# A windowed attention with sinks and a highway layer on one core: last batch loaded in single tokens, loads issued sooner, sinks' keys on GpSimd, sinks' scores in a values' bank, two stretches reordered

## The chip, the core and the metric

The kernel runs on one core of a Trainium2 chip. A core has five engines that matter here, each with an instruction queue of its own that is worked off in order: TensorE (PE in the profile, its weight loads PEld), VectorE (DVE), ScalarE (ACT), GpSimd (POOL) and SyncE (SP). Engines wait for one another by semaphores. Transfers go through 16 DMA engines; they are issued from SP's, ACT's or POOL's queue. The metric is the device time of one execution in microseconds (us); less is better.

## The reference, cut to what matters

Attention over 4 batches, 8 heads, 768 tokens, head size 64, with 4 sinks (the first four keys, which all queries see) and a window of 128 keys; its output, 3,072 tokens of 512 values, goes through a highway layer.

```python
scores = scale * np.matmul(q, k.transpose(0, 1, 3, 2))
keep = is_sink | in_window            # in_window: 0 <= query - key < 128
a = softmax(np.where(keep, scores, -1e9))
x = np.matmul(a, v)                   # then (batch, token) x (head, d): 3072 x 512
H = np.maximum(x @ w_h, 0.0)
T = 1.0 / (1.0 + np.exp(-(x @ w_t + b_t)))
return T * H + (1.0 - T) * x
```

## The kernel before

**Tiles.** 24 token tiles of 128, six for each batch b; tile n is tile t = n mod 6 of its batch. For each tile the work is a chain over engines:

- q and k come from memory by GpSimd's DMAs (`load_part`, L105), are made fp16 on the way, and lie in `nat` with a token per partition: a batch has two halves of 384 tokens, each with 4 loads of q and 4 of k (by groups of heads). In a load, a partition takes 12 tokens that follow one another. VectorE turns blocks of 32x32 (`transpose_qk`, L126), so that head dimension is on partitions: `tr`. As a partition has 12 neighbouring tokens, the result is written with a step of 12 elements between tokens.
- `scores(n)` (L235): TensorE, key tile n against query tiles n and n+1 (only n in a batch's last tile), 16 matmuls into four PSUM banks `ps_s`. `expo(n)` (L266): ScalarE, into E. `mask(n)` (L274): VectorE, in place.
- Tiles with t of 2 and more also need the sinks: `sink_keys(b)` (L215, VectorE, two instructions) puts a batch's first four keys in place, `sink_scores(n)` (L250) makes 4 matmuls of 128x128 into the first 128 columns of `ps_z` (for n of 3 and 4: `ps_h`), `sink_expo(n)` (L257) is ScalarE's exponential of them.
- `values(n)` (L289, L298, L301): TensorE, E times V for tiles n-1 and n, and the sinks, into `ps_v`, one PSUM tile of two banks of 512. `norm(n)` (L310, L311): VectorE, reciprocal of the sums and product: X, fp16.
- `x_transpose(n)` (L338): four TensorE transposes of X into bank 1 of `ps_v`; `x_copy(n)` (L343): ScalarE copies them to XT.
- `bias(n)` and `gate(n)` (L346, L350): TensorE into `ps_z`; `tanh(n)` (L367): ScalarE; the identity 0.5 x + 0.5 behind it on ScalarE for n below 16 and the last two tiles (`gate_on_act`, L373), on GpSimd for the others (`gate_value`, L378).
- `hidden(n)` (L383): TensorE into `ps_h`. `diff(n)` (L387) and `gated(n)` (L391): VectorE. `finish(n)` (L396): GpSimd adds X, and SP issues the store.

**The order.** It is written out by hand: the program's text is, for each engine, the order of its queue, and a dependency from each instruction to the one before it on its engine keeps it (`_keep_traced_order`, L19). Semaphores between engines are set by the framework from the tiles that instructions read and write. A stretch written out in full (L471 to L534) starts tiles 0 to 4. Then a loop (L535) of 20 turns, s from 2 to 21, has four tiles in flight: n2 = s+2 gets its scores, n1 = s+1 its values and norm, n0 = s its transposes, gate and hidden, n9 = s-1 its diff, gated and finish. A turn begins

```python
if n2 > 4:
    if n2 % NC >= 2:
        sink_scores(n2)
        sink_expo(n2)
    x_transpose(n0)
    x_copy(n0)
    scores(n2)
bias(n0)
```

and goes on with `expo(n2)`, `gate_value(n9)`, `diff(n9)`, `mask(n1)`, `gated(n9)`, `finish`, the turn's loads, its VectorE transposes of later q and k (`pieces`), `sink_keys` in a batch's first turn, the first half of the gate, `values(n1)`, `norm(n1)`, the second half, `tanh(n0)` and `hidden(n0)`. Turns in this text are named by n2: 4 to 23. What is loaded in which turn stands in the table `loads` (`put`, L436 to L444), what VectorE transposes in `transposed` (L417 to L422). A stretch after the loop (L574 to L604) ends tiles 21 to 23; the last one is worked in two halves of 256 columns.

Of the kernel before, what the change touches and what calls it, by code (L numbers as in the profile page):

```python
# [32 lines left out]
def kernel(  # L33
# [49 lines left out]


    SEG = 2 * P
    halves = [(0, S // 2), (S // 2, S // 2)]

    segments = [[[(0, SEG), (SEG, S - SEG)], [(0, SEG), (SEG, SEG), (2 * SEG, SEG)]]] + [
        [halves, halves] for b in range(1, B)]
    nat = [[[data.tile([P, HG, nt // 32, D], FP16, tag=f"nat{b}_{t0}_{w}",  # L90
                       name=f"nat{b}_{t0}_{w}") for t0, nt in segments[b][w]]
            for w in range(2)] for b in range(B)]
    tr = [data.tile([P, 2, HG, S, 2], FP16, tag=f"tr{b}", name=f"tr{b}")
          for b in range(B)]

# [9 lines left out]
    def load_part(b, i, g, which, into=None, engine=pool):  # L105
# [5 lines left out]
            in_=(q, k)[which][b, :, t0:t0 + nt, :].rearrange(  # L111
                "(g hg) (r m) d -> g r hg (m d)", g=G, m=nt // 32)[g])

    def part_loads(b, i, which):

        return [lambda g=g: load_part(b, i, g, which) for g in range(G)]

    def segment_loads(b, i):
        return part_loads(b, i, 0) + part_loads(b, i, 1)

    def transpose_qk(b, i, which, lo, hi):

        t0, nt = segments[b][which][i]
        dst = tr[b].bitcast(FP32).rearrange("p w hg t e -> p w hg (t e)")[
            :, which, :, t0:t0 + nt].rearrange("p hg (r m) -> p hg m r", m=nt // 32)
        dve.transpose(out=dst[:, :, lo:hi, :],  # L126
                      in_=nat[b][which][i].bitcast(FP32)[:, :, lo:hi, :])

    def load_v(n):
        b, t = divmod(n, NC)  # L130
# [79 lines left out]
                       base=NSINK - 1, pattern=[[NSINK, H]], channel_multiplier=-1)  # L210


    def sink_keys(b):
        for hg in range(HG):
            dve.tensor_tensor(  # L215
                out=sk[b][:, hg, :, 0:H * NSINK].rearrange("p e (h s) -> p e h s", s=NSINK),
                in0=tr[b][:, 1, hg, 0:NSINK, :].rearrange("p s e -> p e s").unsqueeze(2)
                .to_broadcast([P, 2, H, NSINK]),
                in1=skmask[:, hg].unsqueeze(1).unsqueeze(3)
                .to_broadcast([P, 2, H, NSINK]), op=ALU.mult)  # L220
# [18 lines left out]


    def sink_bank(n):
        return (ps_h if n in (3, 4) else ps_z)[:, 0:P]

    def sink_scores(n):
        b, t = divmod(n, NC)
# [38 lines left out]
    def values(n):  # L284
        b, t = divmod(n, NC)
        both = av_of(n)
        for i in range(2):
            if t >= 2:
                pe.matmul(both[:, i], lhsT=es[n % 2],  # L289
                          rhs=vs[b][:, HB * i:HB * i + HB, :].rearrange("p h e -> p (h e)"),  # L290
                          start=True, stop=False, skip_group_check=True)
            for j in range(HB):
                h = HB * i + j
                g, hg = divmod(h, HG)
                slot = both[:, i, j * (D + 1):(j + 1) * (D + 1)]
                first = t < 2 and j == 0
                if t > 0:
                    pe.matmul(slot, lhsT=E[n - 1][:, g, hg, P:2 * P], rhs=v_of(n - 1)[:, h, :],  # L298
                              start=first, stop=False, skip_group_check=True)
                    first = False  # L300
                pe.matmul(slot, lhsT=E[n][:, g, hg, 0:P], rhs=v_of(n)[:, h, :],  # L301
                          start=first, stop=True, skip_group_check=True)
# [33 lines left out]
    def x_transpose(n):  # L336
        for kc in range(KC):
            pe.transpose(xt_of(n)[:, kc * P:(kc + 1) * P], flat(X[n])[:, kc * P:(kc + 1) * P],  # L338
                         ident)

    def x_copy(n):
        XT[n] = work.tile([P, KC * P], FP16, tag="XT", name="XT")
        act.copy(out=XT[n], in_=xt_of(n))  # L343
# [4 lines left out]
    def gate(n, cols=ALL, parts=range(KC)):  # L348
        for kc in parts:
            pe.matmul(z_of(n, cols), lhsT=XT[n][:, kc * P:(kc + 1) * P], rhs=wt[:, kc, cols],  # L350
                      start=False, stop=(kc == KC - 1))
# [5 lines left out]
    def outputs(n):  # L357
        TH[n] = work.tile([P, DM], FP16, tag="TH", name="TH")
        DD[n] = work.tile([P, DM], FP16, tag="DD", name="DD")
        O[n] = work.tile([P, DM], FP32, tag="O", name="O")  # L360

    def on_act(n):

        return n < 16 or n >= N - 2

    def tanh(n, cols=ALL, gate_too=True):
        act.activation(out=TH[n][:, cols], in_=z_of(n, cols), func=AF.Tanh, scale=0.5)  # L367
        if gate_too:
            gate_on_act(n, cols)
# [11 lines left out]
    def hidden(n, cols=ALL):  # L381
        for kc in range(KC):
            pe.matmul(h_of(n, cols), lhsT=XT[n][:, kc * P:(kc + 1) * P], rhs=wh[:, kc, cols],  # L383
                      start=(kc == 0), stop=(kc == KC - 1))

    def diff(n, cols=ALL):
        dve.scalar_tensor_tensor(out=DD[n][:, cols], in0=h_of(n, cols), scalar=0.0,  # L387
                                 in1=flat(X[n])[:, cols], op0=ALU.max, op1=ALU.subtract)
# [2 lines left out]
        return dve.tensor_tensor(out=DD[n][:, cols], in0=DD[n][:, cols], in1=TH[n][:, cols],  # L391
                                 op=ALU.mult)

    def finish(n, cols=ALL, engine=pool, queue=sp, after=None):

        ins = engine.tensor_tensor(out=O[n][:, cols], in0=DD[n][:, cols],  # L396
                                   in1=flat(X[n])[:, cols], op=ALU.add)
        if after is not None:
            tc.add_manual_dep(
                ins.ins, after.ins.name,  # L400
                mybir.DependencyInfo(
                    mybir.DependencyClass.Sync, mybir.DependencyReason.DATA),
                reason="not beside it")
        queue.dma_start(out=out[n * P:(n + 1) * P, cols], in_=O[n][:, cols])

# [4 lines left out]
    def transposed(b, i, parts, steps):  # L412
        for part, n in zip(parts, steps):
            pieces[n] += [(b, i, *p) for p in part]
# [3 lines left out]
    transposed(1, 1, [[(0, 0, 8), (0, 8, 12)], [(1, 0, 8), (1, 8, 12)]], (7, 8))  # L418
    transposed(2, 0, half_1, (9, 10, 11))
    transposed(2, 1, half_2, (12, 13, 14))  # L420
    transposed(3, 0, half_1, (15, 16, 17))
    transposed(3, 1, half_2, (18, 19, 20))  # L422

    loads = {n: ([], []) for n in range(N)}

    def put(parts, counts):
        parts = list(parts)
        for n, behind, count in counts:
            for i in range(count):
                loads[n][behind].append(parts.pop(0))  # L430
        assert not parts
# [4 lines left out]
    loads[3][0].extend([lambda: load_v(4), lambda: load_v(5)])  # L436
    loads[4][1].append(lambda: load_v_heads(1, 0, H))
    put(segment_loads(1, 1), ((4, 1, 3), (5, 1, 3), (6, 1, 2)))
    put(segment_loads(2, 0), ((6, 1, 2), (7, 1, 4), (8, 1, 2)))
    put(v_halves(2), ((8, 1, 1), (9, 1, 1)))  # L440
    put(segment_loads(2, 1), ((9, 1, 2), (10, 1, 4), (11, 1, 2)))
    put(segment_loads(3, 0), ((11, 1, 2), (12, 1, 4), (13, 1, 2)))
    put(v_halves(3), ((13, 1, 1), (14, 1, 1)))
    put(segment_loads(3, 1), ((14, 1, 1), (15, 1, 4), (16, 1, 3)))  # L444

    loads[17][1].append(lambda: sink_values(3))

# [22 lines left out]

    dve.tensor_copy(out=nat[0][1][0], in_=first[1])  # L471
    transpose_qk(0, 0, 1, 0, 8)
    sink_keys(0)
    act.copy(out=nat[0][0][0][:, 1], in_=first[0][:, 1])
    dve.tensor_copy(out=nat[0][0][0][:, 0], in_=first[0][:, 0])
    transpose_qk(0, 0, 0, 0, 8)
# [40 lines left out]
    hidden(0)  # L517
    x_transpose(2)
    x_copy(2)
    diff(0)  # L520
    transpose_qk(0, 2, 1, 0, 8)
    gated(0)
    for load in loads[3][0]:
        load()
# [7 lines left out]
    expo(4)  # L532
    gate_on_act(1)
    hidden(1)  # L534
    for s in range(2, N - 2):  # L535

        n2, n1, n0, n9 = s + 2, s + 1, s, s - 1
        if n2 > 4:
            if n2 % NC >= 2:
                sink_scores(n2)  # L540
                sink_expo(n2)
            x_transpose(n0)
            x_copy(n0)
            scores(n2)
        bias(n0)
        if n2 > 4:
            expo(n2)
        gate_value(n9)
        diff(n9)
        if n1 > 3:  # L550
            mask(n1)
        last = gated(n9)
        for load in loads[n2][0]:
            load()
        for n in finished.get(n2, (n9,)):
            finish(n, after=last if n2 < 7 else None)
        for load in loads[n2][1]:
            load()
        for piece in pieces[n2]:
            transpose_qk(*piece)  # L560
        if n2 >= NC and n2 % NC == 0:
            sink_keys(n2 // NC)
        if n2 == N - 1:
            finish(n9, after=mask(n2))
        outputs(n0)

        gate(n0, parts=range(0, 2))
        values(n1)
        norm(n1)
        gate(n0, parts=range(2, KC))  # L570
        tanh(n0)
        hidden(n0)
# [14 lines left out]
    x_copy(n1)  # L587
    tanh(n0)
    hidden(n0)
    diff(n0)  # L590
    gated(n0)
    finish(n0)
    outputs(n1)
    for cols in HALVES:
        bias(n1, cols)
        gate(n1, cols)
        tanh(n1, cols)
    for cols in HALVES:
        hidden(n1, cols)
        diff(n1, cols)  # L600
    for cols in HALVES:
        gated(n1, cols)
    finish(n1, HALVES[0], engine=pool)
    finish(n1, HALVES[1], engine=dve, queue=act)  # L604

    _keep_traced_order(tc)
# [33 lines left out]
```

## Time and profile before

| what | value |
|---|---|
| median of 3 runs | 120.95 us (120.65 to 121.06) |
| the profiled execution, its own time | 120.54 us |
| its span, first to last instruction | 118.4 us |
| mean granted TensorE clock | 0.997 |
| busy: PE, DVE, ACT, POOL | 102.2, 98.3, 92.2, 84.5 us |
| DMA packets | 35,023, 17.52 MB; 26,433 of them under 512 B |
| queue of GpSimd's DMAs (q0) | 30,608 packets, 82.7% of 16 engines' span |
| one `x_copy` (L343), mean | 575 ns |
| one exponential of 128x2048 (L266), mean | 1,965 ns |
| one VectorE transpose of 128x512 and of 128x256 (L126), mean | 1,085 and 612 ns |
| issue of one q or k load, of one half of a batch's V, on GpSimd | about 0.55 and 1.44 us |

The span of the profile lies between the first and the last instruction; the execution's own time has some 2 us around it. A busy share is an average over stages with different limits, so what a stage is worth is read from the stage: from the chain of waits (the work that ended last, followed back), from the timeline of one engine in a stretch (start, duration, line; in brackets how long the engine was idle before and what ended that), and from tables of busy time for stretches. Ends of matmuls in the profile are modelled, and one group's end may lie up to 0.16 us behind the next one's start. The trace also has, for every load, the times at which it landed, and the packets of each DMA queue with their sizes.

### The profile page before, as it was taken

Reading aid. Unit: us, or ns where it says so; the run is one execution under the profiler, and the core shown is the slowest. Engines: PE = TensorE matmul, PEld = TensorE weight load, DVE = VectorE, ACT = ScalarE, POOL = GpSimd, SP = SyncE. Lnnn points to the kernel's source line nnn. Section 1 sums busy time; section 2 is a strip of 40 time slices with the busy share of each in tenths; the row PEclk is TensorE's granted clock in tenths of the full one; section 3 lists DMA queues with packets and bytes.
Section 4 is the critical chain, followed back from the end, with each engine's and each line's share of the span. In section 5 each row is a group of like instructions: output and inputs, shape, how many; then the busy total and the mean of one; then the engine's idle time right before and its main releaser. Section 6 shows DMA issues by size and latency. Waiting matters only on the chain.

```text
span 118.4 us, 3080 instructions
## 1 busy us (share of the span) xinstructions
PE 102.2 (86%) x1189; PEld 55.8 (47%) x1189; DVE 98.3 (83%) x194; ACT 92.2 (78%) x118; POOL 84.5 (71%) x119
## 2 busy tenths in 40 slices
PE   5987868879769879999997999999989999999910
PEld 1333445435435445556463454655544556555700
DVE  5679875846997899999979998999999996697580
ACT  0985789769649989999697999897969987863730
POOL 7969999699398996798789696975554435415360
PEclk9999999999999999999999999999999999999998
DMA  3999999999999999899999789999320222022132
GB/s 108 237 204 139 133 167 200 162 144 127 131 149 252 297 191 161 163 164 172 189 233 192 142 166 183 162 228 200 115 89 0 89 94 89 0 94 89 59 118 89
DMA packets 35023, 17.52 MB, mean 148 GB/s; under 512 B 26433, under 2 KB 31297, under 8 KB 35010
## 3 DMA queue, kind: packets, MB, share of 16 engines
q0 software_dynamic: 30608, 9.97, 82.7%
q1 hardware_dynamic: 3938, 6.72, 16.6%
q10 hardware_dynamic: 464, 0.66, 2.1%
q8 instruction: 9, 0.15, 0.5%
q14 instruction: 4, 0.03, 0.1%
HBM read 21.01 MB, written 6.29 MB: 231 GB/s over the span
## 4 chain that ended last, share of the span: by engine, by line
PE 37%; DMA 21%; DVE 16%; issue 8%; ACT 7%; POOL 6%; ACTq 1%; DVEq 0%
PE ps_z L350 9%; DMA wh<-in_moe_w_h_dram 8%; PE ps_h L383 7%; DMA nat<-in_q_dram 5%; DMA first<-in_q_dram 5%; DVE tr L126 4%; PE ps_s L235 4%; POOL nat L109 4%; DVE X L311 4%; ACT E L266 3%; PE ps_v L301 3%; DVE DD L387 3%; DMA v<-in_v_dram 3%; PE ps_v L338 3%; PE ps_z L346 2%
## 5 line engine op out<-in xcount | busy, mean ns | idle before, releaser
L266 ACT ACTIVATE E<-ps_s,ebias 128x2048 f16<-128x2048 f32 (+1 forms) x24 | 43.7, 1822 | 3.0 <-PE ps_s L235 3.0
L396 POOL TENSOR_TENSOR O<-DD,X 128x512 f32<-128x512 f16 (+1 forms) x24 | 27.2, 1135 | 24.3 <-DVE DD L391 12.7
L350 PE MATMUL ps_z<-wt,XT 128*128 128x512 f16 (+1 forms) x96 | 27.6, 375 | 0.3
L126 DVE STREAM_TRANSPOSE tr<-nat 128x512 f32<-128x512 f32 (+1 forms) x30 | 25.5, 896 | 0.8 <-DMA nat<-in_q_dram 0.6
L383 PE MATMUL ps_h<-wh,XT 128*128 128x512 f16 (+1 forms) x96 | 24.2, 375 | 0.4 <-DMA wh<-in_moe_w_h_dram 0.4
L274 DVE TENSOR_TENSOR E<-E,mask_std 128x2048 f16<-128x2048 f16 (+1 forms) x20 | 22.2, 1109 | 0.3 <-ACT E L266 0.2
L387 DVE SCALAR_TENSOR_TENSOR DD<-ps_h,X 128x512 f16<-128x512 f32 (+1 forms) x24 | 16.2, 676 | 4.8 <-PE ps_h L383 3.7
L367 ACT ACTIVATE TH<-ps_z 128x512 f16<-128x512 f32 (+1 forms) x24 | 14.0, 585 | 5.3 <-PE ps_z L350 4.9
L109 POOL DMA_DIRECT2D nat<-in_k_dram x32 | 17.7, 564 | 0.5 <-DMA v<-in_v_dram 0.5
L343 ACT COPY XT<-ps_v 128x512 f16<-128x512 f16 x23 | 13.2, 575 | 5.7 <-PE ps_v L338 5.7
L311 DVE TENSOR_TENSOR X<-ps_v,rec 128x512 f16<-128x512 f32 x23 | 15.9, 691 | 1.1
L109 POOL DMA_DIRECT2D nat<-in_q_dram x28 | 15.5, 560 | 1.2 <-DMA wh<-in_moe_w_h_dram 1.1
L235 PE MATMUL ps_s<-tr 32*128 32x256 f16 (+1 forms) x384 | 14.3, 264 | 2.1 <-DVE mask L477 1.0
L301 PE MATMUL ps_v<-v,E 128*128 128x65 f16 x184 | 15.4, 195 | 0.7 <-DVE E L274 0.6
L298 PE MATMUL ps_v<-v,E 128*128 128x65 f16 x152 | 15.0, 193 | 0.1
L383 PEld LDWEIGHTS <-XT 128*128 128x128 f16 x100 | 9.6, 98 | 11.0 <-issue 0.7
L301 PEld LDWEIGHTS <-E 128*128 128x128 f16 x192 | 12.2, 97 | 5.3 <-DVE E L274 3.7
L373 ACT ACTIVATE TH<-TH,half 128x512 f16<-128x512 f16 (+1 forms) x19 | 13.3, 699 | 0.6
L338 PE MATMUL ps_v<-ident,X 128*128 128x128 f16 x92 | 9.0, 220 | 5.5 <-DVE X L311 5.4
L298 PEld LDWEIGHTS <-E 128*128 128x128 f16 x160 | 12.5, 98 | 2.3 <-issue 0.2
L176 PE MATMUL ps_h<-zeros 128*128 128x512 f16 x36 | 10.3, 442 | 1.3 <-DVE zeros L179 1.3
L391 DVE TENSOR_TENSOR DD<-DD,TH 128x512 f16<-128x512 f16 (+1 forms) x25 | 10.4, 418 | 1.3 <-ACT TH L373 1.3
(70 smaller groups left out, 117.9 us busy)
## 6 DMA issues: line engine op xcount, KB each, us to landing
out_dram<-O SPq DMA_DIRECT2D x23, 256.0 KB, 3.6
nat<-in_q_dram POOLq DMA_DIRECT2D x24, 96.0 KB, 5.3
nat<-in_k_dram POOLq DMA_DIRECT2D x24, 96.0 KB, 4.1
v<-in_v_dram POOLq DMA_DIRECT2D x4, 384.0 KB, 7.8
v<-in_v_dram POOLq DMA_DIRECT2D x6, 128.0 KB, 5.2
v<-in_v_dram POOLq DMA_DIRECT2D x1, 768.0 KB, 10.7
nat<-in_q_dram POOLq DMA_DIRECT2D x4, 128.0 KB, 5.2
nat<-in_k_dram POOLq DMA_DIRECT2D x8, 64.0 KB, 6.9
```

The source lines that it names most:

```text
L109: engine.dma_start(out=into[32 * g:32 * g + 32].rearrange("p hg m d -> p hg (m d)"), in_=(q, k)[which][b, :, t0:t0 + nt, :].rearrange("(g ...
L126: dve.transpose(out=dst[:, :, lo:hi, :], in_=nat[b][which][i].bitcast(FP32)[:, :, lo:hi, :])
L235: pe.matmul(ps_s[:, g, hg, 0:nq * P], lhsT=tr[b][rows, 1, hg, c * P:(c + 1) * P, e], rhs=tr[b][rows, 0, hg, c * P:(c + nq) * P, e], start= ...
L266: act.activation(out=E[n][:, :, :, 0:nq * P], in_=ps_s[:, :, :, 0:nq * P], func=AF.Exp, bias=ebias, scale=SCALE)
L274: return dve.tensor_tensor(out=e3, in0=e3, in1=m[:, 0:nq * P].unsqueeze(1).to_broadcast([P, H, nq * P]), op=ALU.mult)
L298: pe.matmul(slot, lhsT=E[n - 1][:, g, hg, P:2 * P], rhs=v_of(n - 1)[:, h, :], start=first, stop=False, skip_group_check=True)
L301: pe.matmul(slot, lhsT=E[n][:, g, hg, 0:P], rhs=v_of(n)[:, h, :], start=first, stop=True, skip_group_check=True)
L311: dve.tensor_tensor(out=X[n], in0=av[:, :, :, 0:D], in1=rec.unsqueeze(3).to_broadcast([P, 2, HB, D]), op=ALU.mult)
L350: pe.matmul(z_of(n, cols), lhsT=XT[n][:, kc * P:(kc + 1) * P], rhs=wt[:, kc, cols], start=False, stop=(kc == KC - 1))
L383: pe.matmul(h_of(n, cols), lhsT=XT[n][:, kc * P:(kc + 1) * P], rhs=wh[:, kc, cols], start=(kc == 0), stop=(kc == KC - 1))
L387: dve.scalar_tensor_tensor(out=DD[n][:, cols], in0=h_of(n, cols), scalar=0.0, in1=flat(X[n])[:, cols], op0=ALU.max, op1=ALU.subtract)
L396: ins = engine.tensor_tensor(out=O[n][:, cols], in0=DD[n][:, cols], in1=flat(X[n])[:, cols], op=ALU.add)
```

## The change

- **Last batch in single tokens.** q and k of batch 3 no longer come in halves but in 8 loads (4 of q, 4 of k) into one tile `whole`; partition r of a group takes tokens r, r+32, r+64 and so on, so each load has 32 x 48 runs of 64 values instead of 32 x 2 of 768. VectorE transposes it by token tiles: `transpose_tile(n)`, one instruction of 128x512 for q and k of tile n, with neighbouring tokens written side by side. The first one waits for all 8 loads. They stand in turns 16 to 21 for tiles 18 to 23; before, there were four of 128x512 and four of 128x256 in turns 15 to 20.
- **Loads sooner.** In turns 7 to 13 more loads, and none of q or k behind turn 13 (table in the diff).
- **Sinks' keys** of batches 1 to 3 on GpSimd, behind the turn's `finish` and loads; those of batch 0 stay on VectorE.
- **Sinks' scores** of tiles from 5 on go to bank 0 of `ps_v`, and stand behind X's transposes and copy; those of 3 go to `ps_h`, of 2 and 4 to `ps_z`.
- **Fifth step** (turn 4 and what is ahead of it): two VectorE transposes and a norm move ahead of `diff(0)`, `diff(1)` and `gated(1)`.
- **End.** The identity of tile 22 goes to GpSimd; the last tile's second half loses its identity on ScalarE and is finished with two fused VectorE operations.

```diff
+    RUNS = B - 1
+    whole = data.tile([P, 2, HG, S // 32, D], FP16, tag="whole", name="whole")
...
+    def load_whole(g, which):
+        pool.dma_start(
+            out=whole[32 * g:32 * g + 32, which].rearrange("p hg m d -> p (hg m) d"),
+            in_=(q, k)[which][B - 1].rearrange(
+                "(g hg) (m r) d -> g r (hg m) d", g=G, r=32)[g])
...
+    def transpose_tile(n):
+        b, t = divmod(n, NC)
+        dst = tr[b].bitcast(FP32).rearrange("p w hg t e -> p (w hg) (t e)")
+        src = whole.bitcast(FP32).rearrange("p w hg m d -> p (w hg) (m d)")
+        dve.transpose(out=dst[:, :, t * P:(t + 1) * P], in_=src[:, :, t * P:(t + 1) * P])
...
-    def sink_keys(b):
+    def sink_keys(b, engine=pool):
         for hg in range(HG):
-            dve.tensor_tensor(
+            engine.tensor_tensor(
...
     def sink_bank(n):
-        return (ps_h if n in (3, 4) else ps_z)[:, 0:P]
+        return {2: ps_z, 3: ps_h, 4: ps_z}.get(n, ps_v[:, 0])[:, 0:P]
...
     def on_act(n):
-        return n < 16 or n >= N - 2
+        return n < 16 or n == N - 1
...
-    transposed(3, 0, half_1, (15, 16, 17))
-    transposed(3, 1, half_2, (18, 19, 20))
+    tiles = {n: [n + 2] for n in range(RUNS * NC - 2, N - 2)}
...
-    put(segment_loads(2, 0), ((6, 1, 2), (7, 1, 4), (8, 1, 2)))
+    put(segment_loads(2, 0), ((6, 1, 2), (7, 1, 5), (8, 1, 1)))
     put(v_halves(2), ((8, 1, 1), (9, 1, 1)))
-    put(segment_loads(2, 1), ((9, 1, 2), (10, 1, 4), (11, 1, 2)))
-    put(segment_loads(3, 0), ((11, 1, 2), (12, 1, 4), (13, 1, 2)))
+    put(segment_loads(2, 1), ((8, 1, 1), (9, 1, 2), (10, 1, 5)))
+    put([lambda which=which, g=g: load_whole(g, which)
+         for which in range(2) for g in range(G)], ((11, 1, 3), (12, 1, 3), (13, 1, 2)))
     put(v_halves(3), ((13, 1, 1), (14, 1, 1)))
-    put(segment_loads(3, 1), ((14, 1, 1), (15, 1, 4), (16, 1, 3)))
...
+    transpose_qk(0, 2, 1, 0, 8)
     diff(0)
-    transpose_qk(0, 2, 1, 0, 8)
     gated(0)
...
     hidden(1)
+    for piece in pieces[4]:
+        transpose_qk(*piece)
     for s in range(2, N - 2):
         n2, n1, n0, n9 = s + 2, s + 1, s, s - 1
         if n2 > 4:
+            x_transpose(n0)
+            x_copy(n0)
             if n2 % NC >= 2:
                 sink_scores(n2)
                 sink_expo(n2)
-            x_transpose(n0)
-            x_copy(n0)
             scores(n2)
...
         diff(n9)
-        if n1 > 3:
+        if n2 == 4:
+            outputs(n0)
+            gate(n0, parts=range(0, 2))
+            values(n1)
+            norm(n1)
+        else:
             mask(n1)
         last = gated(n9)
...
     hidden(n0)
+    gate_value(n0)
     diff(n0)
...
-    for cols in HALVES:
+    for i, cols in enumerate(HALVES):
         bias(n1, cols)
         gate(n1, cols)
-        tanh(n1, cols)
+        tanh(n1, cols, gate_too=(i == 0))
     for cols in HALVES:
         hidden(n1, cols)
-        diff(n1, cols)
-    for cols in HALVES:
-        gated(n1, cols)
-    finish(n1, HALVES[0], engine=pool)
-    finish(n1, HALVES[1], engine=dve, queue=act)
+    diff(n1, HALVES[0])
+    gated(n1, HALVES[0])
+    finish(n1, HALVES[0])
+    cols = HALVES[1]
+    diff(n1, cols)
+    dve.scalar_tensor_tensor(out=DD[n1][:, cols], in0=TH[n1][:, cols], scalar=1.0,
+                             in1=DD[n1][:, cols], op0=ALU.add, op1=ALU.mult)
+    dve.scalar_tensor_tensor(out=O[n1][:, cols], in0=DD[n1][:, cols], scalar=0.5,
+                             in1=flat(X[n1])[:, cols], op0=ALU.mult, op1=ALU.add)
+    act.dma_start(out=out[n1 * P:(n1 + 1) * P, cols], in_=O[n1][:, cols])
```

More of the change, by code (lines that the diff above doesn't have):

```diff
@@ L85 @@
     SEG = 2 * P
+    RUNS = B - 1
     halves = [(0, S // 2), (S // 2, S // 2)]
     segments = [[[(0, SEG), (SEG, S - SEG)], [(0, SEG), (SEG, SEG), (2 * SEG, SEG)]]] + [
-        [halves, halves] for b in range(1, B)]
+        [halves, halves] for b in range(1, RUNS)]
     nat = [[[data.tile([P, HG, nt // 32, D], FP16, tag=f"nat{b}_{t0}_{w}",
                        name=f"nat{b}_{t0}_{w}") for t0, nt in segments[b][w]]
-            for w in range(2)] for b in range(B)]
+            for w in range(2)] for b in range(RUNS)]
+    whole = data.tile([P, 2, HG, S // 32, D], FP16, tag="whole", name="whole")
     tr = [data.tile([P, 2, HG, S, 2], FP16, tag=f"tr{b}", name=f"tr{b}")
@@ L392, in gated, with finish @@
                                  op=ALU.mult)
-    def finish(n, cols=ALL, engine=pool, queue=sp, after=None):
-        ins = engine.tensor_tensor(out=O[n][:, cols], in0=DD[n][:, cols],
+    def finish(n, cols=ALL, after=None):
+        ins = pool.tensor_tensor(out=O[n][:, cols], in0=DD[n][:, cols],
                                    in1=flat(X[n])[:, cols], op=ALU.add)
@@ L403, in finish @@
                 reason="not beside it")
-        queue.dma_start(out=out[n * P:(n + 1) * P, cols], in_=O[n][:, cols])
+        sp.dma_start(out=out[n * P:(n + 1) * P, cols], in_=O[n][:, cols])
     half_1, half_2 = [[(0, 0, 8)], [(1, 0, 8)], [(0, 8, 12), (1, 8, 12)]], [
@@ L472 @@
     transpose_qk(0, 0, 1, 0, 8)
-    sink_keys(0)
+    sink_keys(0, engine=dve)
     act.copy(out=nat[0][0][0][:, 1], in_=first[0][:, 1])
@@ L558 @@
             load()
-        for piece in pieces[n2]:
-            transpose_qk(*piece)
+        if n2 > 4:
+            for piece in pieces[n2]:
+                transpose_qk(*piece)
+        for n in tiles.get(n2, ()):
+            transpose_tile(n)
         if n2 >= NC and n2 % NC == 0:
@@ L564 @@
             finish(n9, after=mask(n2))
[L565 to L569, printed above, removed]
+        if n2 > 4:
+            outputs(n0)
+            gate(n0, parts=range(0, 2))
+            values(n1)
+            norm(n1)
         gate(n0, parts=range(2, KC))
```

## The prediction

> **What bounds the kernel now.** I read the busy shares first (PE 86%, DVE 83%, ACT 78%): averages, which name no bound. Then the table of busy time for single turns of the loop. A turn is called by its newest token tile, n2; `hidden(n0)` (L383) is its last work on TensorE.
>
> ```profile
> core 0: us, PE busy (x) PEld busy (x) DVE busy (x) ACT busy (x) POOL busy (x), PEclk, DMA share, GB/s
> 49.24:53.28 4.04, 4.04 (x54) 2.37 (x52) 3.87 (x8) 4.01 (x6) 3.54 (x5) 1.00 1.72 146
> 99.38:103.35 3.97, 3.97 (x53) 2.34 (x52) 3.06 (x5) 3.31 (x4) 1.77 (x2) 1.00 0.17 66
> ```
>
> The first row is one turn from the middle, the second one near the end. TensorE is busy in all of both. In the middle ScalarE (4.01 of 4.04 us) and VectorE (3.87) are as full; near the end they have room. The granted clock is 1.00. So a wait put on TensorE is paid in full. The chain of waits for the second row's turn shows its links; the times are those from one group's end to the next one's.
>
> ```profile
> 99.49 0.27 PE ps_z L250 x4
> 99.77 0.22 PE ps_v L338 x4
> 99.99 0.57 PE ps_s L235 x16
> 100.56 0.32 PE ps_z L346
> 100.88 0.47 PE ps_z L350 x2
> ...
> 102.17 0.43 PE ps_z L350 x2
> 102.60 0.86 PE ps_h L383 x4
> ```
>
> These are the sinks' scores (L250), X's transposes (L338), the scores, the bias, half the gate, (left out) the values, the other half and `hidden`: no idle time. The timeline of ScalarE for the middle turn:
>
> ```profile
> 50.58 0.60 ACT L367 ACTIVATE TH<-ps_z 128x512 f16<-128x512 f32 x1
> 51.20 0.72 ACT L373 ACTIVATE TH<-TH,half 128x512 f16<-128x512 f16 x1
> 51.83 0.34 ACT L257 ACTIVATE es<-ps_z,ebias 32x128 f16<-32x128 f32 x1
> 52.08 0.56 ACT L343 COPY XT<-ps_v 128x512 f16<-128x512 f16 x1
> 52.55 1.95 ACT L266 ACTIVATE E<-ps_s,ebias 128x2048 f16<-128x2048 f32 x1
> ...
> 88.48 0.58 ACT L343 COPY XT<-ps_v 128x512 f16<-128x512 f16 x1 [1.02 <-PE ps_v L338]
> ```
>
> One follows the other without a gap. The last line, from a later turn, gives a hand-over: the transposes end at 88.44, the copy starts 0.04 later. The other way, TensorE's gate starts 0.05 after the copy it waits for (81.12 to 81.17). VectorE idles early on:
>
> ```profile
> 26.57 0.69 DVE L387 SCALAR_TENSOR_TENSOR DD<-ps_h,X 128x512 f16<-128x512 f32 x1 [1.51 <-PE ps_h L383]
> 28.15 0.42 DVE L391 TENSOR_TENSOR DD<-DD,TH 128x512 f16<-128x512 f16 x1 [0.89 <-ACT TH L373]
> 28.49 1.08 DVE L126 STREAM_TRANSPOSE tr<-nat 128x512 f32<-128x512 f32 x1
> 29.42 0.16 DVE L310 RECIPROCAL rec<-ps_v 128x8 f32<-128x8 f32 x1
> ...
> 61.79 1.09 DVE L126 STREAM_TRANSPOSE tr<-nat 128x512 f32<-128x512 f32 x1 [0.58 <-DMA nat<-in_q_dram]
> ```
>
> 2.4 us of idle time in turn 4, ahead of the norm that turn 5 waits for, and 0.58 us for a load in turn 12.
>
> **The sinks' scores.** This part decides. In the changed program the first sink matmul carries a wait on ScalarE, for the copy of X's transposes (L343) *of the same turn*: the copy reads `ps_v[:, 1]`, the scores now write `ps_v[:, 0]`, and the two banks are one tile. Before, it waited for the tanh, long over. Queued behind it on TensorE is the whole turn: scores, bias, gate, values, `hidden`; for these wait the exponential, the norm and the tanh. 13 turns have it: 5, 8 to 11, 14 to 17, 20 to 23.
>
> The turn by TensorE, from start to start: `hidden` 0.86, transposes to their end 0.39, hand-over 0.03, copy 0.58, hand-over 0.05, sinks 0.23, scores 0.57, bias 0.22, gate 0.43, values 0.77, gate 0.43 = **4.56 us** against 3.97. Where ScalarE also does the gate's identity (up to turn 17), the copy comes behind it: tanh starts 0.21 after `hidden`, then 0.62 and 0.63 to the copy, its 0.58, hand-over 0.05 (2.09), and 2.65 for sinks to gate = **4.74 us** against 4.03. In each batch's last turn (11, 17, 23) the scores cover one block of queries, 0.2 less. The sinks' exponential now stands behind the copy and waits for the sinks, so ScalarE also idles about 0.6 us per turn: no cover is left for the wait. What it gives back: the bias no longer waits for that exponential, and the gate's and values' short stalls (0.1 each) vanish; the sums above have them out.
>
> **The fifth step (turn 4).** VectorE's idle time takes the key transposes that stood behind it. `transpose_qk(0, 2, 1)` goes ahead of `diff(0)`; its loads land at 22.7, so it runs 23.10 to 24.19. The sinks' scores of 4 move to `ps_z` and wait for the tanh (24.36): 24.41; scores 24.64 (24.86 before), `hidden(1)` 25.20. The transpose at 28.49 moves ahead of `diff(1)`; the queries land at 25.18, so 25.2 to 26.3, and `diff(1)` 26.3. The values end at 27.58, and the norm, now ahead of `gated(1)`, gives X at 28.54 instead of 30.32. Turn 5: transposes 28.7, copy (behind ScalarE's identity) to 29.88, sinks, scores, values once the mask is done (31.1), `hidden(3)` 32.35 instead of 33.12. VectorE has its three transposes done at 32.8, X at 33.7 instead of 35.05: from turn 6 on **-1.35 us**.
>
> **Loads sooner.** The last query part of batch 2 is issued first in turn 10, so 0.58 us go in turn 12. Next late there is the mask, 0.1 behind, so I count 0.5. Cost of issuing: GpSimd's queue is in order with `finish` in it, which has four buffers and no one near behind it.
>
> **Sinks' keys on GpSimd.** VectorE loses 0.35, 0.31 and 0.65 us in turns 6, 12 and 18. In 6 it idled 0.78 behind them: nothing. In 12 and 18 they stood ahead of the norm, but with the longer turns the norm waits for the values: 0.2 together. GpSimd's price lies between 0.25 us each (VectorE's row) and 0.67 (its own 128x256 add); I take 0.35. They stand behind `finish` and the loads: done by 68.1 in turn 12, read at 69.4.
>
> **Last batch in single tokens.** 16 loads of 64 runs become 8 of 1,536 runs of 128 B. Issue: 0.55 us for 64 runs, 1.44 for V's 3,072, so 1.0 each: 8.0 us against 8.8 on GpSimd. Transfer: V's two halves moved 6,097 packets between 70 and 78 us, 760 per us, so 12,288 take 16 us; the 1,024 of 1,536 B take 11 at the 90 per us of 58 to 60 us. From 61 on they land at 77 to 80; the first reader, in turn 16, comes at 79.9 in my schedule. I count nothing, by a hair. VectorE's transposes: 4 of 1,085 ns and 4 of 612 (6.8 us) become 6 of the same 128x512; the writes are now contiguous, and no row has such a one. Bounds: 0.43 us (L475's contiguous cast of that size) to 1.09; I take 1.085, the row of the same operation. They matter only in turns 18 and 19: up to 0.5 us less.
> The Trainium skill (SBUF — State Buffer, "Door 1: The DMA port swizzle") says that each access that crosses into a new 16-byte line pays. The rows (1.85 ns per element of 4 B, all in writes 32 B and more apart) agree so far; by it the transposes would be the cheaper ones and the sum 0.5 us less.
>
> **The end.** The identity of tile 22 goes to GpSimd (0.62 instead of 0.72, hand-overs on both sides): `gated(22)` 0.1 sooner. For the last half, ScalarE's 0.51 falls away; VectorE's line is then serial: 112.50 + diff 0.43, gated 0.43, diff 0.43, two fused operations of 0.43, hand-overs 0.05: 114.7 against 114.96. **-0.25**, from -0.5 to +0.2 (the last one took 0.85 beside GpSimd's).
>
> **Sum.** Start of `hidden` against before, turn by turn: 5: -0.8; 6, 7: -1.35; 8: -0.4 and 9: 0.0 (X came late there, so the transposes' start stays, and copy and sinks come on top); 10: +0.7; 11: +1.2; 12: +1.1; 13: +0.6 (load and keys); 14: +1.5; 15: +1.9; 16: +2.6; 17: +3.1; 18: +3.0; 19: +2.8; 20: +3.8 (X late again); 21: +4.4; 22: +5.0; 23: +5.35. With the end: **+5.1**. The profiled execution took 120.54 us (span 118.4); it lies 0.4 below the median of 120.95. 120.54 + 5.1 = 125.6, or 126.0 on the median; I give **125.7**.
>
> **Rivals.**
> *A, faster: the wait costs nothing*, if the copy is over before TensorE gets there, or the two banks' work overlaps after all. Then remain -1.35 (start), -0.5 (load), -0.5 (keys, in front of the norm again) and -0.25 (end), and 1 us or more for the new loads, which would be read at about 77: 120.54 - 1.6 = 119. For it: PE's end times are modelled. Against: the transposes end 0.1 us before ScalarE is free even now, and a copy of 0.58 cannot be over. It decides from a wait below 0.2 us per turn on. 10%.
> The Trainium skill (Perfetto Trace Analysis, "Matmuls") says that matmul groups should rotate through PSUM banks so that ScalarE's reading of one overlaps the next; by that the change would be A. No row of before shows a matmul beside a read of its tile's other bank.
> *B, the new loads land late*: 590 packets per us (3,072 between the landings 54.4 and 59.8) would land them at 82 to 83; VectorE stalls in turn 16, with the norm behind: up to +2.5, so 127 to 128. For it: DMA is 90% busy there. 14%.
> *C, part is absorbed*: TensorE's ends are modelled up to 0.16 us behind the next group's start; if as much falls away at both ends of the wait, 13 x 0.3 = 3.9 of the +5.1 go: +1.2, 122. 6%.
> The forecast: 70%.
>
> **Chances.** 0.3% is about what a measurement of this kernel can tell. Faster: A, 0.10; within: a part of C, 0.02; slower: 0.88. Range 122.5 to 128.0: it leaves out A and a part of B and C.
>
> **What would show it.** Right: TensorE's sink matmuls in `ps_v` begin 0.05 us after L343's copy, with 0.6 us idle ahead of them, 13 times; turns of 4.6 to 4.7 us; ScalarE idle ahead of the sinks' exponential; X of tile 3 near 28.5; no wait for `whole`. Wrong: sink matmuls right behind the transposes, or turns of 4.0 us.

## The result and the profile after

The changed kernel takes **127.69 us** (median of 4 runs, 126.86 to 128.59) against 121.0 us (120.65 to 121.64): ratio **1.055** (1.045 to 1.065). The forecast was 125.7 us, range 122.5 to 128.0, slower with 88%. Medians here and below are over all runs of a kernel, ratios over undisturbed runs alone, so the two can differ a little.

In the changed program the lines have other numbers: sinks' scores L265 (L250 before), X's transposes L353 (L338), copy L358 (L343), scores L250 (L235), bias and gate L361 and L365, `hidden` L398 (L383). The busy time by stretch, columns as before, each turn here from one start of `hidden` to the next: first a middle turn (10), then a late one (22), then a piece of turn 8:

```profile
52.83:57.61 4.78, 3.96 (x52) 2.33 (x51) 4.07 (x7) 4.04 (x6) 3.63 (x5) 1.00 1.38 136
105.62:110.29 4.67, 3.95 (x53) 2.34 (x51) 3.06 (x6) 3.49 (x5) 1.77 (x2) 1.00 0.15 56
44.30:47.70 3.40, 3.40 (x39) 1.89 (x37) 2.16 (x4) 2.33 (x2) 2.75 (x4) 0.51 1.07 218
```

The same work of about 3.96 us on TensorE now lies in turns of 4.78 and 4.67 us: 0.8 and 0.7 us of it idle. The third row is something else: for 3.4 us TensorE's clock was granted at half (0.51). The chain of waits through a late turn says what the idle time is:

```profile
101.16 0.86 PE ps_h L398 x4
102.02 0.24 PE ps_v L353 x4
102.26 0.02 issue
102.28 0.59 ACT XT L358
102.88 0.04 issue
102.92 0.39 PE ps_v L265 x4
103.31 0.57 PE ps_s L250 x16
103.88 0.32 PE ps_z L361
104.20 0.43 PE ps_z L365 x2
```

Before, the sinks' scores, the transposes, the scores and the bias followed each other on TensorE with nothing between. Now ScalarE's copy (L358) stands in the chain, behind the transposes and ahead of the sinks. The list of waits (who waited for whom: us in total, times, longest) has it 13 times, in its second line:

```profile
DVE rec L325 <- PE ps_v L316: 10.4, 13, 1.6
PE ps_v L265 <- ACT XT L358: 9.9, 13, 1.0
ACT es L272 <- PE ps_v L265: 6.4, 13, 0.5
...
ACT E L281 <- PE ps_s L250: 4.5, 12, 1.2
```

ScalarE's timeline in the middle turn, which had no gap before:

```profile
53.03 0.60 ACT L382 ACTIVATE TH<-ps_z 128x512 f16<-128x512 f32 x1
53.66 0.72 ACT L388 ACTIVATE TH<-TH,half 128x512 f16<-128x512 f16 x1
54.29 0.57 ACT L358 COPY XT<-ps_v 128x512 f16<-128x512 f16 x1
55.34 0.36 ACT L272 ACTIVATE es<-ps_v,ebias 32x128 f16<-32x128 f32 x1 [0.48 <-PE ps_v L265]
55.92 1.97 ACT L281 ACTIVATE E<-ps_s,ebias 128x2048 f16<-128x2048 f32 x1 [0.23 <-PE ps_s L250]
```

After the copy it idles 0.48 us for the sinks and 0.23 for the scores: 0.71 in this turn. VectorE in the fifth step:

```profile
25.83 1.08 DVE L134 STREAM_TRANSPOSE tr<-nat 128x512 f32<-128x512 f32 x1 [0.63 <-DMA nat<-in_q_dram]
26.86 0.69 DVE L402 SCALAR_TENSOR_TENSOR DD<-ps_h,X 128x512 f16<-128x512 f32 x1
28.27 0.21 DVE L325 RECIPROCAL rec<-ps_v 128x8 f32<-128x8 f32 x1 [0.73 <-PE ps_v L316]
28.52 0.69 DVE L326 TENSOR_TENSOR X<-ps_v,rec 128x512 f16<-128x512 f32 x1
```

X of tile 3 is ready at 29.21 (28.52 and 0.69) instead of 30.32; the forecast has 28.54. Of the 0.67 us between, 0.36 are a later start of turn 4 in this execution (28.44 against 28.08). The reordered transpose waited 0.63 us for its query load, but that has no part in it: behind it VectorE idled another 0.73 us for the values (L316). The other 0.31 us lie with these and the norm: the values' modelled end lies 0.26 us ahead of turn 4's start, where the forecast has them end at 27.58, 0.50 ahead of the start before.

### The profile page after: what moved, and what is told of

Same layout as the page of the kernel before. It is cut to its first block, busy times and chain, and to the rows that moved or that the text cites. A ratio compares the mean times of both kernels' runs of the same rounds, so it can differ in the third digit from the quotient of the medians.

```text
span 126.4 us, 3064 instructions
## 1 busy us (share of the span) xinstructions
PE 102.8 (81%) x1189; PEld 56.3 (45%) x1189; DVE 98.0 (78%) x186; ACT 93.1 (74%) x116; POOL 85.0 (67%) x118
## 4 chain that ended last, share of the span: by engine, by line
PE 42%; DMA 17%; ACT 17%; DVE 9%; issue 7%; POOL 6%; DVEq 0%; POOLq 0%; ACTq 0%
PE ps_z L365 10%; DMA nat<-in_q_dram 9%; DMA wh<-in_moe_w_h_dram 8%; ACT E L281 8%; PE ps_h L398 8%; PE ps_s L250 7%; ACT XT L358 6%; PE ps_v L265 4%; PE ps_z L361 3%; DVE X L326 3%; PE ps_v L353 3%; ACT TH L382 3%; PE ps_v L316 2%; PE ps_v L313 2%; POOL O L411 2%
## 5 line engine op out<-in xcount | busy, mean ns | idle before, releaser
L365 PE MATMUL ps_z<-wt,XT 128*128 128x512 f16 (+1 forms) x96 | 28.1, 381 | 0.0
L398 PE MATMUL ps_h<-wh,XT 128*128 128x512 f16 (+1 forms) x96 | 24.2, 375 | 1.1 <-DMA wh<-in_moe_w_h_dram 1.1
L134 DVE STREAM_TRANSPOSE tr<-nat 128x512 f32<-128x512 f32 (+1 forms) x22 | 19.0, 913 | 1.1 <-DMA nat<-in_q_dram 0.8
L358 ACT COPY XT<-ps_v 128x512 f16<-128x512 f16 x23 | 13.3, 577 | 6.5 <-PE ps_v L353 6.3
L316 PE MATMUL ps_v<-v,E 128*128 128x65 f16 x184 | 15.7, 197 | 1.2 <-DVE E L289 1.1
L250 PE MATMUL ps_s<-tr 32*128 32x256 f16 (+1 forms) x384 | 14.7, 269 | 0.5 <-ACT E L281 0.5
L398 PEld LDWEIGHTS <-XT 128*128 128x128 f16 x100 | 9.6, 98 | 11.8 <-issue 1.6
L316 PEld LDWEIGHTS <-E 128*128 128x128 f16 x192 | 12.8, 98 | 4.3 <-DVE E L289 3.2
L325 DVE RECIPROCAL rec<-ps_v 128x8 f32<-128x8 f32 x23 | 4.5, 195 | 12.5 <-PE ps_v L316 10.4
L313 PE MATMUL ps_v<-v,E 128*128 128x65 f16 x152 | 14.0, 196 | 0.1
L313 PEld LDWEIGHTS <-E 128*128 128x128 f16 x160 | 12.8, 100 | 2.5 <-issue 0.5
L265 PE MATMUL ps_v<-tr,sk 128*128 128x128 f16 x52 | 5.1, 219 | 9.9 <-ACT XT L358 9.9
L111 POOL DMA_DIRECT2D nat<-in_k_dram x24 | 13.0, 554 | 0.1
L388 ACT ACTIVATE TH<-TH,half 128x512 f16<-128x512 f16 (+1 forms) x17 | 12.0, 709 | 0.5
L111 POOL DMA_DIRECT2D nat<-in_q_dram x20 | 11.2, 566 | 1.9 <-DMA wh<-in_moe_w_h_dram 1.0
L191 PE MATMUL ps_h<-zeros 128*128 128x512 f16 x36 | 11.1, 469 | 1.3 <-DVE zeros L194 1.3
## 6 DMA issues: line engine op xcount, KB each, us to landing
v<-in_v_dram POOLq DMA_DIRECT2D x6, 128.0 KB, 5.7
```

The lines of the kernel that those rows point to most:

```text
L111: engine.dma_start(out=into[32 * g:32 * g + 32].rearrange("p hg m d -> p hg (m d)"), in_=(q, k)[which][b, :, t0:t0 + nt, :].rearrange("(g ...
L134: dve.transpose(out=dst[:, :, lo:hi, :], in_=nat[b][which][i].bitcast(FP32)[:, :, lo:hi, :])
L250: pe.matmul(ps_s[:, g, hg, 0:nq * P], lhsT=tr[b][rows, 1, hg, c * P:(c + 1) * P, e], rhs=tr[b][rows, 0, hg, c * P:(c + nq) * P, e], start= ...
```

## The experiments

The first four kernels shared a chip on which the kernel before took 120.38 us (median of 13), the next four one with 120.57 (29), the last four one with 120.8 (29). Turns are compared by the start of `hidden` counted from that of turn 4, which takes out the start of the program: turn 4's own start lay between 27.66 and 28.91 us in the profiles.

The theory: ps_v's two banks are one tile, so the sinks' first matmul waits for the copy of the same turn, and a turn of TensorE's queue stands behind it. Rivals: the order (sinks behind the transposes) costs the time, whatever the bank; the new loads come late; keys, start or end cost it.

**1. The change with the sinks undone**

```diff
-        return {2: ps_z, 3: ps_h, 4: ps_z}.get(n, ps_v[:, 0])[:, 0:P]
+        return {2: ps_z, 3: ps_h, 4: ps_z}.get(n, ps_z)[:, 0:P]
...
-            x_transpose(n0)
-            x_copy(n0)
             if n2 % NC >= 2:
                 sink_scores(n2)
                 sink_expo(n2)
+            x_transpose(n0)
+            x_copy(n0)
```

> The changed kernel with the sinks' scores of tiles 5 and up back in ps_z and back ahead of X's transposes; all else of the change stays. Theory (the wait for X's copy is the whole loss): the other edits together gain, so about 119 us (118 to 120). Rival (single-token loads, keys on GpSimd or the reordering lose as well): 121.5 or more.

Measured 119.57 us (118.59 to 120.5, 4 runs), ratio 0.985 (0.977 to 0.993). The whole loss is gone, and the rest of the change gains. The interval is wide; experiment 12 repeats the kernel. The windows of its middle and late turn (10 and 22):

```profile
49.15:53.19 4.04, 4.04 (x52) 2.34 (x51) 3.87 (x7) 4.01 (x6) 3.65 (x5) 1.00 1.80 186
96.87:100.84 3.97, 3.97 (x52) 2.33 (x51) 3.06 (x6) 3.27 (x5) 1.79 (x3) 1.00 0.17 68
```

4.04 and 3.97 us, and TensorE is busy in all of both, as before the change.

**2. The sinks' edit alone, on the kernel before**

```diff
-        return (ps_h if n in (3, 4) else ps_z)[:, 0:P]
+        return {2: ps_z, 3: ps_h, 4: ps_h}.get(n, ps_v[:, 0])[:, 0:P]
...
+            x_transpose(n0)
+            x_copy(n0)
             if n2 % NC >= 2:
                 sink_scores(n2)
                 sink_expo(n2)
-            x_transpose(n0)
-            x_copy(n0)
```

> The kernel before with nothing but the sinks' scores of tiles 5 and up in bank 0 of ps_v and behind X's transposes and copy. Theory: 13 waits of 0.6 to 0.7 us, none of the gains: 127 to 129 us. Rival (the loss comes from the edits meeting one another): below 124.

Measured 128.69 us (128.01 to 129.84, 4 runs), ratio 1.070 (1.061 to 1.078); from turn 4 to turn 23 its profile takes 86.45 us against 78.32 before, +8.1. The edit alone loses more than the whole change (1.070 against 1.055): the other parts win back about the 1.5% that they gained in experiment 1.

**3. The order kept, the bank not: sinks behind the transposes, in ps_z**

```diff
-        return {2: ps_z, 3: ps_h, 4: ps_z}.get(n, ps_v[:, 0])[:, 0:P]
+        return {2: ps_z, 3: ps_h, 4: ps_z}.get(n, ps_z)[:, 0:P]
```

> The changed kernel with the sinks' scores in ps_z, but left behind X's transposes and copy; their first matmul then waits for the tanh of the turn before, not for the copy. Theory (the wait, not the place): the bias waits 0 to 0.3 us per turn for the sinks' exponential, 119 to 121.5 us. Rival (the place in the queues costs, whatever the bank): 125 or more.

The four executions took 120.66 us (the profiled one), 122.96, 123.27 and 123.51 (median 123.11). The profiled one lies in the expected range, the others between it and the rival's; no ratio is drawn from them. In the profile a middle turn (10) takes 4.13 us, against 4.78 in the change and 4.04 in experiment 1. So in this execution the order by itself costs about 0.1 us a turn, and the chain of waits in that turn shows how:

```profile
51.90 0.56 ACT XT L358
52.47 0.27 ACT es L272
52.73 0.04 issue
52.77 0.38 PE ps_z L361
```

With the sinks in ps_z, the bias (L361) has to wait for their exponential, which now stands behind the copy. The other 0.65 us of the turn come with the bank. Why the three other executions took 2.3 to 2.9 us more is not known, and by them the order could cost some 3 us in all. What it costs in the change, where the sinks do not share a bank with the bias, is left to experiment 4.

**4. The bank kept, as two tiles:** all as in the change, but ps_v is two tiles of one bank each, and the norm two halves.

```diff
-    ps_v = psum.tile([P, 2, 512], FP32, tag="ps_v", name="ps_v")
+    ps_v = [psum.tile([P, 512], FP32, tag=f"ps_v{i}", name=f"ps_v{i}") for i in range(2)]
...
-        dve.reciprocal(out=rec, in_=av[:, :, :, D])
-        dve.tensor_tensor(out=X[n], in0=av[:, :, :, 0:D],
-                          in1=rec.unsqueeze(3).to_broadcast([P, 2, HB, D]), op=ALU.mult)
+        for i in range(2):
+            dve.reciprocal(out=rec[:, i], in_=av[i][:, :, D])
+        for i in range(2):
+            dve.tensor_tensor(out=X[n][:, i], in0=av[i][:, :, 0:D],
+                              in1=rec[:, i].unsqueeze(2).to_broadcast([P, HB, D]), op=ALU.mult)
```

> The changed kernel with ps_v as two tiles of one bank each, the sinks' scores where the change puts them; the norm becomes two reciprocals and two products, some 0.35 us more of VectorE per turn. Theory (the wait exists because the two banks are one tile): the sink matmuls follow the transposes at once; 120 to 122 us with VectorE's extra. Rival (the banks collide in the hardware, or the place costs): 126 or more.

Measured 120.23 us (118.82 to 122.19, 10 runs), ratio 0.993 (0.988 to 0.998). The timelines of TensorE and of ScalarE in a late turn (some lines have moved by 3: `hidden` is L401 here, the transposes L356, the copy L361):

```profile
97.76 1.03 PE L401 MATMUL ps_h<-wh,XT 128*128 128x512 f16 x4
98.62 0.39 PE L356 MATMUL ps_v<-ident,X 128*128 128x128 f16 x4
98.84 0.39 PE L265 MATMUL ps_v<-tr,sk 128*128 128x128 f16 x4
99.17 0.63 PE L250 MATMUL ps_s<-tr 32*128 32x256 f16 x16
```

```profile
99.09 0.58 ACT L361 COPY XT<-ps_v 128x512 f16<-128x512 f16 x1 [0.47 <-PE ps_v L356]
99.57 0.35 ACT L272 ACTIVATE es<-ps_v,ebias 32x128 f16<-32x128 f32 x1
99.86 1.97 ACT L281 ACTIVATE E<-ps_s,ebias 128x2048 f16<-128x2048 f32 x1
```

Same order, same bank 0, same bank 1: the sinks begin 0.22 us after the transposes' start, before the copy of the other bank has even begun. The wait belonged to the tile, not to the banks. The order, which is that of the change, costs nothing that shows. This settles the cause. The Trainium skill (Perfetto Trace Analysis, "Matmuls") asks for matmul groups that rotate through PSUM banks, so that ScalarE reads one while the next is filled; where the banks are two tiles this trace agrees as far as it goes (sinks from 98.84 to a modelled end at 99.23, copy from 99.09: at most 0.14 us side by side), and where they are one tile the change's trace does not (sinks 0.04 behind the end of the copy). Against experiment 1 (0.985 and, once more below, 0.991) the two tiles gain nothing that shows: where the sinks stood before, TensorE was full already.

**5 to 8. Each other part alone, on the kernel before.** Five is the fifth step, six the single tokens with their loads, seven the keys, eight the end; each is the change's diff for that part.

> The kernel before with nothing but the fifth step's new order (two VectorE transposes and a norm moved ahead). Theory: X of tile 3 1.4 to 1.8 us sooner, 1.35 us from turn 6 on, of which the later turns keep all: 1.0 to 1.4 us below the kernel before. Rival (the moved transposes wait for their loads, or the later turns take it back): within 0.4 us of before.

> The kernel before with nothing but the last batch's loads by single tokens, its transposes by tiles, and the new table of loads. Theory: the stall for a load in turn 12 goes (0.5 us), six transposes of 0.70 us in place of 6.8 us, of which only turns 18 and 19 can use some: 0.4 to 1.0 us below before. Rival (12,288 small packets land late for the first reader): 1 us or more above before.

> The kernel before with nothing but the sinks' keys of batches 1 to 3 on GpSimd. Theory: 0.3 us of VectorE in turn 12 and 0.65 in turn 18 ahead of the norm go: 0.2 to 0.8 us below before. Rival (the keys stand behind finish and loads on GpSimd and come late for the sink matmuls): 0 to 1 us above before.

> The kernel before with nothing but the new end. Theory: 0.25 us below before (0.5 below to 0.2 above), as VectorE's line becomes serial. Rival (ScalarE's part was not what set the end): no difference.

| part alone | median, us | ratio (interval) |
|---|---|---|
| fifth step | 119.48 (5 runs) | 0.988 (0.983 to 0.993) |
| single tokens, loads sooner | 119.73 (12) | 0.992 (0.988 to 0.995) |
| keys on GpSimd | 119.93 (12) | 0.994 (0.991 to 0.998) |
| end | 120.42 (12) | 0.997 (0.994 to 1.000) |

None of them loses, so none is the cause. But 1.2%, 0.8%, 0.6% and 0.3% make 2.9%, or 3.5 us, and all four together (experiment 1) brought 1.5% (0.7 to 2.3). The last four kernels ask whether the gains add.

**9. The change once more**

> The change, unaltered, once more: is the half clock of 3.4 us in turn 8 of its first profile part of it, and how large is the loss without it? Theory (the two-bank tile makes the sinks' matmul wait for the copy in every turn): 6 to 7 us above the before of the same chip, so 126.5 to 127.5, with mid turns of 4.7 to 4.8 us and late ones of 4.6 to 4.7 whatever the clock does. Rival (the half clock comes with the change's longer idle time on TensorE at the start): a stretch of half clock in this profile too, and 127.5 to 128.5.

Measured 127.98 us (126.59 to 128.75, 6 runs), ratio 1.058 (1.052 to 1.064). That is 7.2 us above the kernel before, a little more than the 6 to 7 expected. No half clock this time, against the rival. Turn 8, and the same middle and late turn as above:

```profile
41.25:47.19 5.94, 3.91 (x50) 2.12 (x49) 5.77 (x10) 3.93 (x6) 5.42 (x10) 1.00 1.12 260
52.15:56.93 4.78, 3.96 (x52) 2.33 (x51) 4.07 (x7) 4.04 (x6) 3.44 (x5) 1.00 1.86 177
104.95:109.62 4.67, 3.95 (x53) 2.34 (x52) 3.06 (x6) 3.50 (x5) 1.77 (x2) 1.00 0.15 56
```

Turn 8 takes 5.94 us instead of 7.26, so the half clock cost 1.3 us there in the first profile. Turn 9 gave 0.2 of it back (4.77 us instead of 4.96), and the turns from 10 on are the same to 0.01 us: 1.1 us are left at the end. What sets off the half clock stays open: the longest idle time of TensorE ahead of it, the one for X, is no shorter in the execution that kept the full clock (1.36 us against 1.17), and no other profile here has half the clock between turns 4 and 23.

**10. Experiment 1 with all keys on VectorE**

```diff
-    def sink_keys(b, engine=pool):
+    def sink_keys(b, engine=dve):
```

> The change with the sinks' scores back in the bank of z, ahead of the transposes of X, and the sinks' keys of every batch on VectorE as before. It tells what the keys on GpSimd bring beside the other edits. If they bring what they bring alone: 0.3 to 0.7 us above the version that has them on GpSimd in this same set of runs. Rival (with the other edits they come 0.4 us late to the sinks' matmul, and VectorE has no queue to shorten): no difference, or up to 0.3 us below that version.

Measured 119.52 us (118.68 to 120.58, 12 runs), ratio 0.992 (0.989 to 0.995).

**11. Fifth step and single tokens together**

> The kernel before with two parts of the change: the reordered start (fifth step) and the last batch in single tokens with its loads issued sooner. Keys and end as before, sinks' scores in the bank of z. If the two gains add (1.4 and 1.0 us, each measured alone): 118.0 to 118.4. If they do not add: 118.8 to 119.6, and then the hidden starts show the start's gain by turn 6 and the same turns of 3.97 us as before in the last batch.

Measured 119.55 us (118.22 to 121.24, 12 runs), ratio 0.989 (0.985 to 0.993).

**12. Experiment 1 once more**

> The change with the sinks' scores back in the bank of z ahead of the transposes of X, once more, beside the others of this set: 118.6 to 119.6, some 1.0 to 1.9 us below the kernel before, and 7 to 8 us below the change as it is. If it comes out at or above the kernel before, the gain found first was chance.

Measured 119.83 us (118.72 to 121.99, 12 runs), ratio 0.991 (0.987 to 0.995). It is a little above the 118.6 to 119.6 expected. It beats the kernel before and the change; among 1, 4, 5, 10, 11 and 12 the intervals overlap, and no best one can be named.

So the keys do not show beside the other parts (0.992 with them on VectorE, 0.991 without), and the gains do not seem to add: 0.988 and 0.992 would give 0.980, outside the interval of 11 (0.985 to 0.993), though not by much, as the two have errors of their own. VectorE's timelines show one reason, first of 11, then of 10:

```profile
41.11 1.53 DVE L134 STREAM_TRANSPOSE tr<-nat 128x512 f32<-128x512 f32 x2 [0.95 <-DMA nat<-in_q_dram]
...
78.58 0.71 DVE L142 STREAM_TRANSPOSE tr<-whole 128x512 f32<-128x512 f32 x1 [0.33 <-DMA v<-in_v_dram]
```

```profile
40.88 1.53 DVE L134 STREAM_TRANSPOSE tr<-nat 128x512 f32<-128x512 f32 x2 [0.94 <-DMA nat<-in_q_dram]
...
78.65 0.71 DVE L142 STREAM_TRANSPOSE tr<-whole 128x512 f32<-128x512 f32 x1 [0.89 <-DMA v<-in_v_dram]
```

In both the start has gained 1.09 us by turn 7, and by turn 8 all but 0.07 to 0.08 us of it is gone: VectorE reaches the query load before it has landed. In experiment 12 the same load costs 0.16 us, and 0.74 us are left in turn 8. In 10 and 11 the first transpose of `whole` too comes before all has landed and waits 0.89 and 0.33 us. (The view names V's load as the releaser, but that lands only at 81.1 and 81.2; the last load of `whole` lands at 78.42 and 78.36, 0.2 us ahead of the transpose.) In experiment 12 it does not wait: all has landed at 76.39, and it starts at 76.91. Who is sooner at a load that lands when it did waits longer; how late it lands differs from execution to execution (the query load of turn 8 at 40.14 in 12 and at 41.08 in 11). That this is all of the missing 0.9% is not shown.

## Why the prediction was right

**The wait** was the cause (experiments 1, 2 and 4), on the turns named (13 times, and each time the sinks begin 0.05 us behind the end of the copy), and nearly of its size. Turns of 4.74 and 4.56 us were forecast; 4.78 and 4.67 were measured. From turn 8 to 23, with 11 turns that have the wait, experiment 9 takes 66.83 us and experiment 12 takes 59.72: 0.65 us a turn. The terms: hand-overs 0.02 and 0.04 (forecast 0.03 and 0.05), copy 0.59 (0.58), but from the sinks' start to the scores' 0.32 instead of 0.23, in all 13 turns. For the middle turns the forecast named another path than the trace:

```profile
51.15 1.97 ACT E L281
53.12 0.52 ACT TH L382
...
54.29 0.57 ACT XT L358
54.86 0.04 issue
54.91 0.39 PE ps_v L265 x4
55.30 0.60 PE ps_s L250 x16
55.90 0.02 issue
55.92 1.97 ACT E L281
```

The chain runs copy, sinks, scores, exponential, tanh, identity, copy, that is through ScalarE's 1.97 us, and not, as forecast, over the gate and `hidden` on TensorE. Both ways come to nearly the same sum: the tanh starts at 57.81, the gate's modelled end lies at 57.77 and the exponential's at 57.89. So that the 4.74 us held is partly luck.

**Too small** were turns 14 to 16: 4.95 to 4.98 us each in experiment 9, +2.41 against before where the forecast has +2.0. X comes late there: VectorE's reciprocal begins 0.4 us behind the values' modelled end in turn 15. The view puts that down to the gate's second half; no experiment took it apart.

| `hidden` after turn 4's, us | turn 7 | 8 | 11 | 17 | 23 |
|---|---|---|---|---|---|
| before | 13.42 | 17.92 | 30.36 | 54.80 | 78.32 |
| forecast, difference | -1.35 | -0.4 | +1.2 | +3.1 | +5.35 |
| change (experiment 9), difference | -1.08 | +0.36 | +2.21 | +4.59 | +6.79 |
| change (first profile), difference | -1.06 | +1.70 | +3.36 | +5.74 | +7.93 |
| experiment 12, difference | -1.09 | -0.74 | -0.73 | -1.02 | -1.42 |

**The start** gave 1.05 to 1.09 us by turn 7 in every profile that has it, not 1.35. What is missing is about what X of tile 3 came late against turn 4's start: 0.77 us behind it in the change and in experiment 12, where the forecast has 0.46. Then turn 8 took back 0.5 us more than forecast, with VectorE waiting for the query load (0.37 us in experiment 9). Over a third of the miss of the total lies there, and as much in the run: turn 4 of experiment 9 began 0.83 us later than in the profile of before, as the load of `hidden`'s weights, which the first `hidden` waits for, landed at 22.3 us instead of 21.4. 5.1 + 0.27 (start) + 0.49 (turn 8) + 0.25 (9 to 11) + 0.43 (12 to 23) + 0.83 is 7.4; the profiled executions differ by 127.76 - 120.54 = 7.2. In the first profile the half clock leaves another 1.1 by turn 23.

**The loads**: rival B, late loads of the last batch, did not happen in the change. All have landed by 79.0, and VectorE reads them first at 82.7, later than forecast since the turns are longer. In the faster versions they are read at 77 to 79, as in rival A: VectorE waits 0.3 to 0.9 us for them in the profiles of experiments 4, 10 and 11 and not at all in those of 1 and 12 (rival A had 1 us or more). One rate in rival B was misread: 3,072 packets between the landings at 54.4 and 59.8 are some 570 per us, not 590; its landing time of 82 to 83 stays. **VectorE's transposes** were mis-sized. The instances of both kinds in the change, from the views of the two lines (shortest, median, longest in ns):

```profile
L134 DVE STREAM_TRANSPOSE tr<-nat x22: 597/1083/1111, 6.2 to 72.9; 128x512 f32<-128x512 f32 x14, 128x256 f32<-128x256 f32 x8
```

```profile
L142 DVE STREAM_TRANSPOSE tr<-whole x6: 702/703/705, 82.7 to 104.1; 128x512 f32<-128x512 f32 x6
```

703 ns with contiguous writes, against 1,085 with a step: inside the bounds of 0.43 to 1.09, but the upper end had been taken. The Trainium skill's rule of the 16-byte lines (SBUF — State Buffer, "Door 1: The DMA port swizzle") had the side of it right. In the change it moved little, since VectorE waits there anyway.

**The keys** took 0.54 to 0.63 us for two on GpSimd in the change, not 0.70 as taken; a gain of 0.2 us was forecast, and nothing shows beside the other parts. **The end** went against its forecast of -0.25: from the start of the last tile's first `hidden` half to VectorE's last end it takes 3.41 us instead of 3.09, as gated and the first fused operation took 0.64 and 0.65 us, not 0.43 (GpSimd works beside them; no experiment shows that this is why). That the profiles show 0.3 us less in all comes from the last store: 2.8 us from its issue to the end of the span against 3.4; experiment 11 has the end as before and shows 2.9, so this is no doing of the edit. The 0.3% of experiment 8 has no cause that the traces show, and its interval reaches 1.000.

**Rival A** was a fair picture of the kernel without the wait: 1.6 us below the kernel before were worked out, and by their ratios experiments 1 and 12 lie 1.8 and 1.1 us below it. **Rival C** did not happen: no part of the wait was absorbed.

## What to carry to other kernels

In this framework a wait is set by the tile, not by the bank: where one instruction reads half of a tile and another writes the other half, ask who waits for whom, and whether the writer stands in front of a full engine's queue; two tiles take the wait away. Undo the suspected part first, and do it alone too: the two runs bracket its price. Gains of parts that end at the same load need not add: after each, look for the next transfer that now lands too late.

## What the runs showed of the hardware

- The two PSUM banks need no wait between TensorE's writing of one and ScalarE's reading of the other: in experiment 4 the sinks' matmuls start before the copy of the neighbour bank, and the copy takes 0.58 us as elsewhere. By the modelled ends the two run side by side for at most 0.2 us, so what a longer overlap costs is not shown.
- A VectorE transpose of 128x512 costs 0.70 us with contiguous writes and 1.085 with a step of 12 elements.
- The same program was granted half the clock for 3.4 us in one profiled execution (0.51) and not in the other, with no longer idle time ahead of it (1.17 against 1.36 us): 1.3 us of difference in that turn that no line of the program explains.
